# Lending a free layer-input block to the attention pipeline: one more buffer of parts, one more of transposed parts, and five units under way instead of four

## The chip, the core and the metric

The kernel runs on one core of one Trainium2 chip. The metric is the device time of one execution in microseconds (us). Five engines share the work: TensorE (PE in the profile; its weight loads are PEld), VectorE (DVE), ScalarE (ACT), GpSimd (POOL) and SyncE (SP). In this program SP issues nearly all transfers, from one queue, in the order in which they stand in it. PSUM is the memory that matmuls write; all else that is named here lies in SBUF.

## What is computed

Attention in which a query sees only keys of its own bucket, for 2 batches of 8 heads, 768 rows of 64 elements; then two layers on the 1536 x 512 result:

```
mask = q_bucket == k_bucket                   # six sign bits of a projection
scores = where(mask, q @ k.T / sqrt(64), -1e9)
attn = softmax(scores);  x = attn @ v          # put together to 1536 x 512
x = elu(x @ w_in) @ w_out                      # layer 1, 512 -> 2048 -> 512
r = relu(x @ w_in2);  y = (s * r * r + b) @ w_out2   # layer 2
```

Values are split into two f16 parts (high and low), and a product takes three f16 matmul passes: high by high, high by low, low by high.

## The kernel before

**Units.** A unit is one head by 128 queries; there are 96, and `u_s` to `u_av` (lines 378 to 441) take one through its steps. `u_s` makes the scores on PE (L384, four matmuls). `u_soft` takes the row minimum on DVE while it copies the scores to a buffer `p` (L395), scales the minimum (L396, on POOL for units 16 to 43), and takes the exponential on ACT (L397). From unit 16 on `u_split` writes the high part of the probabilities on ACT (L416) and the low part on POOL (L419) into a buffer of parts `ph`, which the SP queue transposes into a buffer `pt` (L421, a transfer). `u_av` multiplies `pt` by the values on PE (L440, 18 matmuls). After the eighth unit of a chunk of 128 rows `u_norm` divides by the sums on DVE, splits the result (L475 on POOL makes the low part), and transposes it into a block of layer input `xx[0]`, `xx[1]` or `xx[2]` (L479 for the first two chunks, L482 later). Each block holds four chunks, 8 KB in each of the 128 partitions. `xx[1]` is first written at the end of the fifth chunk, that is after unit 39.

**Buffers and units under way.** A small `Ring` object gives out the buffers of a kind in rotation. From unit 16 (`U0`) there are 3 `p`, 3 `ph` and 4 `pt`, and `attention` (line 518) issues the scores of a unit only while fewer than `nxt["lag"]` units lie between it and the last `u_av`: 4 from unit 16 on. When the stream of layer-1 weights is through, at unit 40 at the latest, `w1_step` adds one buffer of each kind and sets the lag to 5.

**Beside it.** Layer 1 (`moe1`, products at L574) works on blocks of two chunks, so its first block can start when the first two chunks are transposed. Its weights come as 64-bit numbers; `w_stream` loads them (L175 on SP, 512 KB each) and joins and splits them, mostly with four DVE instructions for a chunk (L213, L214, L216, L223). The layer's ELU takes a DVE instruction too (L591).

**What sets the order.** The Python code emits work in one sequence; a scheduler then places each instruction on its engine by priority and by when it reckons its inputs to be ready. Each engine runs its own list strictly in that order. Buffers and the lag enter the reckoning, so a change there moves instructions on all engines.

Of the kernel before, what the change touches and what calls it, by code (L numbers as in the profile page):

```python
# [7 lines left out]
F32 = mybir.dt.float32  # L8
# [10 lines left out]
PT = 4  # L19
EX = dict(p=1, ph=1, pt=1, raw=2)  # L20
NP = 3
# [17 lines left out]
NPH = 3  # L39
# [24 lines left out]
W_FROM = 3  # L64
HOLD = {(0, 2, "v"): 3, (0, 3, "v"): 4, (1, 0, "k"): 8, (1, 0, "q"): 9}
HOLD_E = []
LN2 = 0.6931471805599453


def model_kernel(tc, q, k, v, proj, w_in, w_out, w_in2, w_out2, s2, b2, sel, pop, eye, out):  # L70
    nc = tc.nc
    B, H, S, D = q.shape
# [22 lines left out]
    with ExitStack() as base:  # L95
# [13 lines left out]
        unp = right(ast, "unp", NP)  # L109
        un3 = right(ast, "un3", NPH)  # L110
        ptp = right(ast, "ptp", PT)
# [7 lines left out]
        class Ring:  # L119
            def __init__(self):  # L120
                self.sets, self.n = {}, {}
# [5 lines left out]
            def take(self, kind, shape, dt, name):  # L127
                pools = self.sets[kind]
                self.n[kind] += 1
                tag = "m" if kind == "w" else kind  # L130
                return pools[self.n[kind] % len(pools)].tile(shape, dt, tag=tag, name=name)

        class late_by:
            def __init__(self, n):
# [8 lines left out]
        ring = Ring()  # L143
# [22 lines left out]
        def behind(n):  # L166

            return tc.issue_after(w_loads[n]) if n is not None else nullcontext()
# [9 lines left out]
        def w_early(ch, x):  # L178
            t = xx[1].rearrange("p a t -> p (a t)").bitcast(I32)[:, 1024 * x:1024 * x + 1024]
            with behind(HOLD_E[x]):  # L180
                nc.sync.dma_start(out=t.rearrange("p (k n) -> p k n", k=ch[1].shape[1]), in_=ch[1])
            return ch, t.rearrange("p (n t) -> p n t", t=2)
# [192 lines left out]
        sps, pf, pt, sums, xacc = ({} for _ in range(5))  # L375
# [12 lines left out]
        def u_soft(u):  # L388
# [6 lines left out]
            nc.vector.tensor_scalar(f, sps.pop(u), CLAMP, None, op0=ALU.min, op1=ALU.min, accum_out=mx)  # L395
            (nc.gpsimd if U0 <= u < MXP else nc.vector).tensor_scalar(mx, mx, sm / (SQ * SQ), 10.0 * LN2, op0=ALU.mult, op1=ALU.add)  # L396
            nc.scalar.activation(out=f, in_=f, func=ACTF.Exp, scale=-sm / (SQ * SQ), bias=mx,  # L397
# [26 lines left out]
        def u_av(u):  # L424
            b, c, h, hp, j = unit(u)
            gr, sl = group(u)
            if sl == 0:
                xacc[gr] = ps_x.tile([128, H, D], F32, tag="x", name="xacc")
            acc = xacc[gr][:, sl, :]
            o = pt.pop(u)  # L430
            if u < FC * H:
                vv = raws[b, hp, "v"].rearrange("p h (c d) -> p h c d", d=D)
                for cc in range(C):
                    nc.tensor.matmul(acc, o[:, 128 * cc:128 * cc + 128], vv[:, j, cc, :],  # L434
                                     start=(cc == 0), stop=(cc == C - 1))
                return
            vv = vHL[b, hp]
            for z, (x, y) in enumerate(((0, 0), (0, 1), (1, 0))):
                for cc in range(C):
                    nc.tensor.matmul(acc, o[:, C * x + cc, :], vv[:, j, cc, y, :],  # L440
                                     start=(z == 0 and cc == 0), stop=(z == 2 and cc == C - 1))

        xx = [xs_.tile([128, 2 * KM, 512], F16, name=f"x{i}") for i in range(B * C // 4)]
# [68 lines left out]
        nxt = {"s": 0, "av": 0, "soft": [], "split": [], "lag": LAG0}  # L512
# [5 lines left out]
        def attention():  # L518
            for i in range(-PRE, 0):
                for fn, a in sched.get(i, []):  # L520
                    fn(*a)
                yield
            while nxt["av"] < NU:
                if nxt["split"]:
                    u_split(nxt["split"].pop(0), SPLIT(nxt["s"]))
                u = nxt["av"]
                if u < nxt["s"] and u in pt and (nxt["s"] - u >= nxt["lag"] or nxt["s"] == NU):
                    u_av(u)
                    nxt["av"] += 1
                    if u % H == H - 1:  # L530
                        u_norm(u // H)
                        if u >= FC * H - 1:
                            done_chunks[0] = u // H + 1
                u = nxt["s"]
                if u < NU and u - nxt["av"] < nxt["lag"]:
                    if u == U0:
                        ring.use(p=[unp], ph=[un3], pt=[ptp])
                        nxt["lag"] = PT
                    u_s(u)
                    nxt["s"] += 1  # L540
                    yield
                    u_soft(u)
                    nxt["split"].append(u)
                    for fn, a in sched.get(u, []):
                        fn(*a)
                yield
        att = attention()


# [302 lines left out]
        if True:  # L852
# [12 lines left out]
            n, early = 0, []  # L865
            co1 = w_col_chunks(lambda: wo, w_out)
            for _ in att:
                n += 1
                if len(early) < len(HOLD_E) and len(w_loads) > HOLD_E[len(early)]:
                    early.append(w_early(co1[len(early)], len(early)))  # L870
# [155 lines left out]
```

## Time and profile before

| what | value |
|---|---|
| median of 3 runs | 709.73 us (708.51 to 713.6) |
| profiled execution, its own time | 714.04 us |
| its span in the trace | 711.8 us |
| PE busy in the span | 659.6 us, 93% |
| DVE busy | 520.5 us, 73% |
| ACT busy | 416.3 us, 58% |
| POOL busy | 266.1 us, 37% |
| mean granted PE clock | 0.978 of full speed |

The span is what the trace covers; the execution's own time is 2.24 us longer. The trace's times count from the start of the span. The units that the change touches run from about 88 us (their first scores) to about 160 us (the last of their products). A busy PE is not PE at its peak, and idle time of an engine only costs where someone waits for it.

### The profile page before, as it was taken

The numbers are of one execution on the slowest core, as the hardware profiler recorded it, in microseconds if no ns is written. First come the engines' busy times: TensorE is split into PE (matmuls) and PEld (weight loads), VectorE is DVE, ScalarE is ACT, GpSimd is POOL, SyncE is SP. The second block draws the span as 40 slices with busy tenths as digits, with TensorE's granted clock in tenths as the row PEclk, the third lists the DMA queues.
The fourth block names the chain that finished last, engine by engine and source line by source line (L and its number), as shares of the span: only waits on it lengthen the run. The fifth ranks groups of instructions, "written<-read, shape, count | busy, mean of one in ns | idle before, by whom it ended". The sixth has DMA issues, their size and how long they took to land.

```text
span 711.8 us, 15212 instructions
## 1 busy us (share of the span) xinstructions
PE 659.6 (93%) x6192; PEld 506.6 (71%) x6192; DVE 520.5 (73%) x893; ACT 416.3 (58%) x687; POOL 266.1 (37%) x211
## 2 busy tenths in 40 slices
PE   2598978879989999999999999999999999999998
PEld 0286857668767777888888988874444446888887
DVE  5779989998878568645644699339999626999730
ACT  2849768966778788656755333234545525555520
POOL 0136767776345469945855421311211200000000
PEclk9769999999999999999999999999999999999999
DMA  9965699999999669977668555014443000000100
GB/s 211 299 162 170 160 203 203 223 228 225 196 211 216 116 116 171 150 125 122 119 115 117 135 162 165 1 31 119 135 138 112 0 1 1 16 31 31 45 30 30
DMA packets 206805, 89.72 MB, mean 126 GB/s; under 512 B 171920, under 2 KB 203408, under 8 KB 206736
## 3 DMA queue, kind: packets, MB, share of 16 engines
q1 hardware_dynamic: 206144, 88.63, 57.4%
q8 instruction: 48, 0.79, 0.5%
q14 instruction: 21, 0.17, 0.1%
q10 hardware_dynamic: 592, 0.14, 0.1%
HBM read 43.13 MB, written 3.15 MB: 65 GB/s over the span
## 4 chain that ended last, share of the span: by engine, by line
PE 66%; DMA 10%; DVE 10%; ACT 7%; issue 5%; SPq 1%; POOL 1%; DVEq 0%; ACTq 0%; POOLq 0%
PE h L574 27%; PE y L818 15%; PE x2p L574 12%; DMA pt<-ph 6%; PE s L384 4%; PE xacc L440 3%; PE xacc L434 2%; DVE p L395 2%; ACT p L397 1%; PE pT L406 1%; ACT ph L416 1%; DMA q<-src 1%; DVE g L591 1%; DMA raw<-in_k 1%; ACT q L357 1%
## 5 line engine op out<-in xcount | busy, mean ns | idle before, releaser
L419 POOL TENSOR_TENSOR ph<-p,ph 128x768 f16<-128x768 f32 x80 | 134.6, 1686 | 79.2 <-ACT ph L416 44.3
L574 PE MATMUL h<-x,wih 128*128 128x256 f16 x768 | 131.3, 275 | 3.0 <-DVE g L591 1.5
L574 PE MATMUL h<-x,wi 128*128 128x512 f16 x576 | 124.5, 379 | 0.0
L395 DVE TENSOR_SCALAR_CACHE_REDUCE p<-s 128x768 f32<-128x768 f32 x96 | 91.0, 951 | 42.2 <-PE s L384 41.3
L397 ACT ACTIVATE p<-p,mx 128x768 f32<-128x768 f32 x96 | 89.2, 929 | 50.6 <-DVE mx L396 38.8
L818 PE MATMUL y<-wqh,a 128*128 128x256 f16 x672 | 110.3, 273 | 0.0
L818 PEld LDWEIGHTS <-a 128*128 128x128 f16 x1008 | 98.6, 98 | 11.7
L574 PE MATMUL h<-x,wil 128*128 128x256 f16 x384 | 105.4, 275 | 0.0
L574 PE MATMUL x2p<-gh,woh 128*128 128x256 f16 x384 | 104.1, 273 | 0.8 <-ACT gh L594 0.8
L574 PE MATMUL x2p<-gl,woh 128*128 128x256 f16 x384 | 104.5, 273 | 0.1
L574 PEld LDWEIGHTS <-wi 128*128 128x128 f16 x576 | 56.4, 98 | 67.7
L574 PE MATMUL x2p<-gh,wol 128*128 128x256 f16 x384 | 104.5, 273 | 0.0
L818 PE MATMUL y<-wql,a 128*128 128x256 f16 x336 | 91.1, 273 | 0.0
L384 PE MATMUL s<-k,q 128*128 128x512 f16 (+1 forms) x384 | 80.7, 335 | 8.0 <-DVE p L395 7.9
L574 PEld LDWEIGHTS <-wih 128*128 128x128 f16 x768 | 74.9, 99 | 15.2 <-issue 2.0
L574 PEld LDWEIGHTS <-woh 128*128 128x128 f16 x768 | 74.9, 98 | 11.6
L597 POOL TENSOR_TENSOR gl<-g,gh 128x512 f16<-128x512 f32 x48 | 59.0, 1229 | 61.0 <-ACT gh L594 60.7
L440 PE MATMUL xacc<-vv,pt 128*128 128x64 f16 x1440 | 57.6, 194 | 16.1 <-DMA pt<-ph 16.1
L416 ACT ACTIVATE ph<-p 128x768 f16<-128x768 f32 x80 | 66.7, 836 | 7.7 <-DMA pt<-ph 5.2
L440 PEld LDWEIGHTS <-pt 128*128 128x128 f16 x1440 | 53.5, 99 | 24.3 <-DMA pt<-ph 20.3
L610 DVE SCALAR_TENSOR_TENSOR g<-h,sbs,r 128x512 f32<-128x512 f32 x48 | 35.7, 745 | 23.6 <-ACT r L607 23.6
L384 PEld LDWEIGHTS <-q 128*128 128x128 f16 x384 | 34.5, 100 | 25.6 <-issue 10.8
(118 smaller groups left out, 1040.8 us busy)
## 6 DMA issues: line engine op xcount, KB each, us to landing
wraw<-in_moe_w_in SPq DMA_DIRECT2D x32, 512.0 KB, 3.9
wraw<-in_moe_w_out SPq DMA_DIRECT2D x32, 512.0 KB, 3.9
out<-y SPq DMA_DIRECT2D x10, 256.0 KB, 2.0
raw<-in_k SPq DMA_DIRECT2D x6, 384.0 KB, 4.8
raw<-in_q SPq DMA_DIRECT2D x6, 384.0 KB, 5.7
v<-in_v SPq DMA_DIRECT2D x4, 384.0 KB, 7.8
pt<-ph SPq DMA_TRANSPOSE x80, 4.1
x<-in_k SPq DMA_DIRECT2D x2, 384.0 KB, 5.0
```

What stands on the lines that cost most here:

```text
L357: nc.scalar.activation(out=o[r, j].rearrange("p c t -> p (c t)"), in_=p[r], func=ACTF.Relu, scale=sc, bias=pop_sb[r, x:x + 1])
L384: nc.tensor.matmul(p[:, a0:a1], w[b, hp][:, j, c, :], kf[:, a0:a1], start=(x == 0), stop=(x == 1))
L395: nc.vector.tensor_scalar(f, sps.pop(u), CLAMP, None, op0=ALU.min, op1=ALU.min, accum_out=mx)
L397: nc.scalar.activation(out=f, in_=f, func=ACTF.Exp, scale=-sm / (SQ * SQ), bias=mx, accum_out=sums[gr][:, sl:sl + 1])
L416: nc.scalar.activation(out=t[:, 0, :], in_=f, func=ACTF.Copy)
L419: nc.gpsimd.tensor_tensor(out=t[:, 1, :], in0=f, in1=t[:, 0, :], op=ALU.subtract)
L434: nc.tensor.matmul(acc, o[:, 128 * cc:128 * cc + 128], vv[:, j, cc, :], start=(cc == 0), stop=(cc == C - 1))
L440: nc.tensor.matmul(acc, o[:, C * x + cc, :], vv[:, j, cc, y, :], start=(z == 0 and cc == 0), stop=(z == 2 and cc == C - 1))
L574: nc.tensor.matmul(p, ws[a](kk), xs[b](kk), start=(kk == 0 and z == 0), stop=(kk == n_kk - 1 and z == 2))
L597: nc.gpsimd.tensor_tensor(out=gl, in0=t["g"], in1=gh, op=ALU.subtract)
L610: nc.vector.scalar_tensor_tensor(out=g, in0=p, scalar=sb["s"], in1=t["r"], op0=ALU.mult, op1=ALU.mult)
L818: nc.tensor.matmul(p, a[:, xa, kk, :], wq[y][:, WQ[n], kk, :], start=first and k == 0, stop=k == 3 * K2 - 1, skip_group_check=True)
```

## The change

From unit 16 to unit 33 `Ring` gets a fourth buffer of parts `ph` and a fifth of transposed parts `pt`. Both lie in the block `xx[1]`, 3,072 bytes per partition each (`Guest` gives out a view of it). There is no fourth `p` (`X1["p"]` is 0). The lag is 5 from unit 16 and goes back to 4 at unit 34, when the rotations are set back to what they were. No instruction is added or removed: on each engine as many stand as before.

```
+X1 = dict(p=0, ph=1, pt=1)
+X1_END = 34
...
+        class Guest:
+            def __init__(self, t, at, n):
+                self.t, self.at, self.n = t, at, n
+            def tile(self, shape, dt, tag=None, name=None):
...
+                t = self.t[:, self.at // 2:(self.at + n * z) // 2]
...
                     if u == U0:
+                        t, at_, sets = xx[1].rearrange("p a t -> p (a t)"), 0, {}
+                        for k_, p_, n_ in (("p", unp, NP), ("ph", un3, NPH), ("pt", ptp, PT)):
+                            sets[k_] = [p_] * n_
+                            for _ in range(X1[k_]):
+                                sets[k_].append(Guest(t, at_, 4 * S))
+                                at_ += 4 * S
+                        ring.use(**sets)
+                        nxt["lag"] = PT + X1["pt"]
+                    if u == X1_END:
                         ring.use(p=[unp], ph=[un3], pt=[ptp])
                         nxt["lag"] = PT
```

In the lists below the changed kernel's line numbers are 19 higher for the lines that matter here: its L403, L415, L438, L440, L459, L494 and L498 are L384, L396, L419, L421, L440, L475 and L479 of before, and L194 is L175. A buffer that is written `x1_114` is the lent block.

**PE, where unit 16 comes to its product with the values** (`s` are scores, `k12` and `q12` head pair 2, `pt_967` the transposed parts of unit 16). Before, the end of the scores that stand ahead of it:

```order
L384 LDWEIGHTS q21_199
L384 MATMUL s_1034<-k21_189,q21_199 128x512
L384 LDWEIGHTS q21_199
L384 MATMUL s_1034<-k21_189,q21_199 128x256
L440 LDWEIGHTS pt_967
L440 MATMUL xacc_1094<-vv0_850,pt_967 128x64
```

and with the change:

```order
L403 LDWEIGHTS q12_356
L403 MATMUL s_1047<-k12_347,q12_356 128x512
L403 LDWEIGHTS q12_356
L403 MATMUL s_1047<-k12_347,q12_356 128x256
L403 LDWEIGHTS q22_358
L403 MATMUL s_1047<-k22_348,q22_358 128x512
L403 LDWEIGHTS q22_358
L403 MATMUL s_1047<-k22_348,q22_358 128x256
L459 LDWEIGHTS pt_967
L459 MATMUL xacc_1107<-vv0_850,pt_967 128x64
```

One more unit's scores stand ahead of the first product.

**POOL, where the second chunk's low part is made** (`xh` is the chunk's split result, `ph` or `x1` parts of a unit, `mx` the minimum). Before:

```order
L419 TENSOR_TENSOR ph_991<-p_986,ph_991 128x768
L396 TENSOR_SCALAR mx_1008<-mx_1008 128x1
L475 TENSOR_TENSOR xh_1029<-xf_1027,xh_1029 128x2x256
L396 TENSOR_SCALAR mx_1085<-mx_1085 128x1
L419 TENSOR_TENSOR ph_1012<-p_1007,ph_1012 128x768
L396 TENSOR_SCALAR mx_1133<-mx_1133 128x1
L419 TENSOR_TENSOR ph_1089<-p_1084,ph_1089 128x768
```

and with the change:

```order
L438 TENSOR_TENSOR ph_985<-p_980,ph_985 128x768
L415 TENSOR_SCALAR mx_1002<-mx_1002 128x1
L415 TENSOR_SCALAR mx_1022<-mx_1022 128x1
L438 TENSOR_TENSOR x1_114<-p_1001,x1_114 128x768
L438 TENSOR_TENSOR ph_1026<-p_1021,ph_1026 128x768
L494 TENSOR_TENSOR xh_1042<-xf_1040,xh_1042 128x2x256
```

The chunk's low part now stands behind the low parts of units 18 and 19.

**SP's queue at the same place.** Before:

```order
L421 DMA_TRANSPOSE pt_994<-ph_991 128x12x128
L175 DMA wraw_1178<-in_moe_w_out 128x4x256
L479 DMA_TRANSPOSE x0_113<-xh_1029 128x4x128 x2
L421 DMA_TRANSPOSE pt_1015<-ph_1012 128x12x128
L421 DMA_TRANSPOSE pt_1092<-ph_1089 128x12x128
```

and with the change:

```order
L440 DMA_TRANSPOSE pt_988<-ph_985 128x12x128
L194 DMA wraw_1191<-in_moe_w_out 128x4x256
L440 DMA_TRANSPOSE pt_1008<-x1_114 128x12x128
L194 DMA wraw_1293<-in_moe_w_out 128x4x256
L440 DMA_TRANSPOSE x1_114<-ph_1026 128x12x128
L498 DMA_TRANSPOSE x0_113<-xh_1042 128x4x128 x2
```

The chunk's two transposes into the layer input now stand behind two unit transposes and one more weight load.

## Rows read from the trace of the kernel before

**Rows 1.** The page: span and busy time of each engine.
```profile
span 711.8 us, 15212 instructions
PE 659.6 (93%) x6192; PEld 506.6 (71%) x6192; DVE 520.5 (73%) x893; ACT 416.3 (58%) x687; POOL 266.1 (37%) x211
```
**Rows 2.** Stretches: length, busy time by engine, granted PE clock, DMA share, GB/s.
```profile
110.00:155.00 45.00, 39.07 (x473) 31.90 (x470) 44.53 (x74) 37.55 (x68) 35.84 (x34) 1.00 1.06 213
155.00:170.00 15.00, 12.64 (x134) 9.98 (x133) 11.27 (x22) 9.53 (x18) 10.21 (x11) 0.89 1.13 242
170.00:181.00 11.00, 11.00 (x163) 9.73 (x162) 10.07 (x18) 6.08 (x11) 3.45 (x3) 1.00 1.12 202
181.00:300.00 119.00, 109.53 (x1321) 88.70 (x1317) 87.23 (x169) 98.79 (x168) 75.47 (x53) 1.00 0.93 168
300.00:445.00 145.00, 145.00 (x1662) 126.86 (x1661) 94.32 (x183) 75.92 (x130) 69.50 (x49) 1.00 0.65 132
```
**Rows 3.** Waits from 95 to 180 us: total us, times, longest.
```profile
PE xacc L440 <- DMA pt<-ph: 9.0, 7, 2.4
ACT ph L416 <- DMA pt<-ph: 2.8, 4, 1.1
```
**Rows 4.** Waits of SP's queue from 95 to 180 us, the first two.
```profile
SPq L421 <- POOL mx L396: 20.7, 11, 3.0
SPq L421 <- POOL ph L419: 8.0, 6, 2.1
```
**Rows 5.** PE in order of time: start, length, instruction, [idle before <- releaser].
```profile
97.09 1.14 PE L440 MATMUL xacc<-vv,pt 128*128 128x64 f16 x18 [2.01 <-DMA pt<-ph]
...
103.17 0.39 PE L574 MATMUL h<-x,wih 128*128 128x256 f16 x2 [1.48 <-DMA x<-xh]
...
160.17 0.70 PE L440 MATMUL xacc<-vv,pt 128*128 128x64 f16 x18 [2.36 <-DMA pt<-ph]
```
**Rows 6.** POOL in order of time: the second chunk's low part, unit 19's low part.
```profile
95.84 1.16 POOL L475 TENSOR_TENSOR xh<-xf,xh 128x512 f16<-128x512 f32 x1 [1.09 <-DVE xh L474]
...
99.69 1.65 POOL L419 TENSOR_TENSOR ph<-p,ph 128x768 f16<-128x768 f32 x1
```
**Rows 7.** SP's queue in order of time: the second chunk's transposes.
```profile
97.33 2.88 SPq L479 DMA_TRANSPOSE x<-xh  x2
```
**Rows 8.** PE in order of time: three units' scores, two units' products with the values.
```profile
90.88 2.11 PE L384 MATMUL s<-k,q 128*128 128x512 f16 x12
...
107.32 1.21 PE L440 MATMUL xacc<-vv,pt 128*128 128x64 f16 x36
```
**Rows 9.** DVE in order of time: the row minimum before unit 16's product, and waits.
```profile
95.67 0.95 DVE L395 TENSOR_SCALAR_CACHE_REDUCE p<-s 128x768 f32<-128x768 f32 x1
...
161.32 0.96 DVE L395 TENSOR_SCALAR_CACHE_REDUCE p<-s 128x768 f32<-128x768 f32 x1 [1.42 <-PE s L384]
...
167.62 0.96 DVE L395 TENSOR_SCALAR_CACHE_REDUCE p<-s 128x768 f32<-128x768 f32 x1 [1.45 <-PE s L384]
```
**Rows 10.** PE alone, slices of 1 us: length, busy, granted clock, DMA share, GB/s.
```profile
161.00:162.00 1.00, 1.00 (x7) 0.77 1.10 246
162.00:163.00 1.00, 1.00 (x17) 0.50 0.70 165
163.00:164.00 1.00, 1.00 (x12) 0.50 1.01 332
164.00:165.00 1.00, 1.00 (x7) 0.52 1.22 237
```
**Rows 11.** A slice of 0.5 us, columns as in rows 2.
```profile
143.00:143.50 0.50, 0.50 (x7) 0.45 (x5) 0.50 (x2) 0.00 (x0) 0.46 (x1) 1.00 1.28 284
```
**Rows 12.** Waits from 181 to 300 us.
```profile
PE xacc L440 <- DMA pt<-ph: 7.0, 7, 1.7
```
**Rows 13.** PE in order of time: layer products, three matmuls apart.
```profile
103.83 0.38 PE L574 MATMUL h<-x,wih 128*128 128x256 f16 x2
...
104.16 0.38 PE L574 MATMUL h<-x,wih 128*128 128x256 f16 x2
```

More of the change, by code (lines that the diff above doesn't have):

```diff
@@ L131, in take @@
                 return pools[self.n[kind] % len(pools)].tile(shape, dt, tag=tag, name=name)
+        class Guest:
+            def __init__(self, t, at, n):
+                self.t, self.at, self.n = t, at, n
+            def tile(self, shape, dt, tag=None, name=None):
+                z = 4 if dt == F32 else 2
+                n = 1
+                for d in shape[1:]:
+                    n *= d
+                assert n * z <= self.n
+                t = self.t[:, self.at // 2:(self.at + n * z) // 2]
+                t = t.bitcast(F32) if z == 4 else t
+                if len(shape) == 3:
+                    t = t.rearrange("p (a b) -> p a b", a=shape[1])
+                return t
         class late_by:
```

## The prediction, made before the changed kernel ran

> **What bounds the kernel now.** I read the page first. PE is busy 659.6 of 711.8 us and no other engine comes near [rows 1], so the time is PE's work plus the time in which PE stands still or runs at its lower clock. The change adds and removes no instruction; it can only move PE's idle time. The second view, busy time by stretch, says where there is any: from 300 to 445 us PE is busy for all of 145.00 us; from 110 to 155 it idles 5.9 of 45 us, from 155 to 170 2.4 of 15, from 170 to 181 not at all, from 181 to 300 9.5 of 119 [rows 2]. The lent buffers serve units 16 to 33, whose products with the values (L440) run from 97.09 to 160.17 us [rows 5], 17 unit periods of 3.71 us. So I look at that stretch, and then at what it hands on.
>
> The third view is the waits. Between 95 and 180 us PE waited seven times, 9.0 us in all, for a unit's transposed parts, at most 2.4 us [rows 3]; the first of these, 2.01 us at 97.09, is unit 16's own, whose transfer is issued as before [rows 5], so 7.0 us are open to the change. ACT waited four times, 2.8 us, for a free buffer of parts [rows 3]. The long waits of the transposes on SP's queue end with POOL's work, not with a product that frees a `pt` [rows 4]. So the fourth `ph` has a direct price in this trace, 2.8 us of ACT, and ACT is not full (37.55 of 45 us, rows 2); the fifth `pt` has none. What is left is the deeper pipeline: a product that comes later than its transpose.
>
> DVE is the other thing to see. From 110 to 155 us it is busy 44.53 of 45 us [rows 2]: there row minima and weight splitting are the pace, and units can't come faster than DVE passes them. From 155 to 170 it idles 3.7 us, of which 1.42 and 1.45 us are waits for scores [rows 9] that stand on PE behind the product that came late at 160.17.
>
> **The change part by part.**
>
> *Lead of the scores.* The lag goes up by one unit, but what counts is how many units' scores stand ahead of a product in PE's list. I counted that in both orders for units 16 to 33: before, 4.25 to 6, with the change 5 to 7; for units 17 to 33 the mean goes from 5.29 to 5.65. A product gets 0.36 unit, 1.3 us at 3.71 us a unit, more time for its transpose, not a unit. At unit 33, the late one, the lead goes from 4.5 to 5, 1.9 us.
>
> *Unit 16's product* now stands behind a fifth unit's scores. They need the minimum before them, which ends at 95.67 + 0.95 = 96.62 [rows 9], and take a third of 2.11 us [rows 8], so PE is through at 97.3 instead of having waited until 97.09 [rows 5]: +0.2 us, below what I can resolve; it counts as part of the next term.
>
> *The start of layer 1.* The second chunk's low part ran on POOL at 95.84 [rows 6], SP issued its transposes at 97.33 [rows 7], and PE's layer products had them at 103.17 after a wait of 1.48 us [rows 5]. Now the low part stands behind those of units 18 and 19, and unit 19's can't end before 99.69 + 1.65 = 101.34 [rows 6]. With 1.16 us for itself, SP gets the issue at 102.5 instead of 97.33: 5.2 us later, so the layer's products wait for 103.17 + 5.2 = 108.4 us. PE has more to do before them now: two more units' scores (2/3 of 2.11) and two products (1.21, rows 8) come from behind to ahead of them, 2.6 us. Idle there becomes 1.48 + 5.2 - 2.6 = 4.1 instead of 1.48: +2.6, with the fifth scores **+2.8 us**. Ends: 0, if the low parts of units 18 and 19 come sooner than they did, and +5.2 with none of the moved work in the gap, plus 1.7 for the clock (next) if the idle is long enough to lower it.
>
> *From 110 to 155 us.* 7.0 - 2.4 = 4.6 us of PE's waits for transposes lie here. What I weigh is whether they come back. The row of the stretch has DVE idle for 0.5 us [rows 2]; a unit that waits less for its transpose is still handed on at DVE's pace, so PE would stand at the next scores. I take **0**; the ends are -4.6 (all of it filled by layer products that stand in between) and +0.5 (the DVE slack lost too). The Trainium skill, Perfetto Trace Analysis, Identifying Performance Opportunities, says that improvement comes from the most-contended engine. By that rule the stretch gives nothing, since the change touches no DVE work; by PE's wait rows alone it would give 4.6.
>
> *From 155 to 170 us.* Unit 33's product waited 2.36 us [rows 5]. With 1.9 us more lead 0.5 is left. Behind that wait the granted clock fell from 2.4 to 1.2 GHz: 0.77 in the slice from 161 us, 0.50 in the next two, 0.52 in the one from 164 [rows 10], so 0.23 + 0.5 + 0.5 + 0.48 = 1.7 us of work lost; from 110 to 155 us, where the waits are shorter, the clock stays at 1.00 [rows 2]. DVE has 3.7 us of room here, so the gain can be kept. **-3.6 us.** Ends: 0 and -4.1.
>
> *From 181 us on.* The rotations are as before from unit 34, all lists are reshuffled, the work is the same. PE waits 7.0 us for transposes here [rows 12], and these can fall either way: **0**, ends -3.5 and +3.5 by half of that row.
>
> *Sum:* +2.8 + 0 - 3.6 + 0 = -0.8 us. Against the profiled execution's own 714.04 that is 713.2; that execution lies 4.3 above the median of 709.73, and above all three timed runs, so against the median I forecast **708.9 us**.
>
> **The rivals.**
>
> *The waits were a shortage of buffers.* All six remaining waits shrink by the 1.3 us of lead: the five before 155 us, 0.9 us each in the mean, vanish (4.6), the longest loses 1.3; the fall of the clock goes with them, 1.7; and the layer's start costs nothing. Then 709.73 - 7.6 = **702.1 us**. For it: the waits repeat, product after product, on the engine that should be full, and ACT's 2.8 us point to buffers too. Against it: DVE's 44.53 of 45. The Trainium skill, Perfetto Trace Analysis, Consistent bubbles under Identifying Performance Opportunities, reads a gap that repeats on the engine that should be saturated as a possible sign of too few buffers; the trace has such gaps, but no transpose that waited for a `pt`.
>
> *The queue takes the gain.* The DMA share is 1.06 and 1.13 in the two stretches [rows 2], and a slice in which transfers run without a gap has 1.28 [rows 11]. Units that come earlier find the weight loads in front of them, transposes only land later, and the product waits as long. Then only the start's 2.8 us are left: **712.5 us**. For it: 83% to 88% of that best slice. Against it: the 12% to 17% left.
>
> *Attention stays at DVE's pace and layer 1 falls behind: slower.* In PE's new order there are 24 to 64 fewer layer matmuls ahead of the scores of a given unit from the thirtieth on; at the sixtieth, whose scores lie in the last part of the stretch to 300 us, 758 instead of 803. If attention runs no faster, these 45 are done later, and from 300 us on PE is full and nothing hides them [rows 2]. Three take 0.33 us [rows 13], so 45 cost 4.95; with one more fall of the clock at the layer's start, 1.7, the time is 709.73 + 6.65 = **716.4 us**. It decides if attention reaches the sixtieth unit less than about 4 us sooner than before. For it: DVE full to 155 us. Against it: DVE's 3.7 us of room from 155 to 170, and near the end of attention the new order is only 12 matmuls behind.
>
> *The change doesn't do what it says* is half true already (0.36 unit of lead instead of one) and is in the forecast.
>
> **How the numbers follow.** Forecast, about 709 us: 0.47. Buffers, 702.1: 0.20. Queue, 712.5: 0.18. Layer behind, 716.4: 0.15. A measurement of this kernel can tell about 1% from no change, here 702.6 and 716.8. Faster by over 1%: half of the buffers' case and a little of the forecast's lower tail, 0.14. Slower by over 1%: half of the layer's case and the upper tails, 0.11. Within 1%: 0.75. All cases but the outer halves of the two extreme ones, with the ends of the terms, give 701 to 715.5 us as the range for 8 in 10.
>
> **What would show it.** In the new trace: the first long wait of layer products should end near 108 us, not 103, with 4 us of idle before it; if it ends by 104, the start's term is wrong. The waits of L440 between 110 and 155 us should shrink, while PE's idle time there stays near 6 us and moves to other releasers, with DVE still full; if PE's idle falls by 4, the DVE term is wrong. The wait near unit 33 should be under 1 us, with no clock of 0.5 behind it. PE's idle time up to 300 us, against that of before, tells the sum. It would be wrong altogether if a new fall of the clock, or a new order of the second batch's preparation after 181 us, moved more than 4 us.

## The result, and the profile after

The change is **slower by 1.0%**: 718.64 us (median of 8, 717.09 to 722.71) against 711.76 us for the kernel before (median of 8 beside it), ratio 1.0104 with the interval 1.0070 to 1.0138. The forecast was 708.9. Of the 9.7 us between, 2.0 lie in the level of before (709.73 in the three runs shown, 711.76 in eight) and 7.7 in the sum: -0.8 forecast, +6.9 measured.

The profiled execution of the change took 720.25 us, 6.2 more than that of before. Its page answers to [rows 1]:

```profile
span 718.5 us, 15207 instructions
PE 661.7 (92%) x6192; PEld 503.8 (70%) x6192; DVE 519.2 (72%) x893; ACT 415.4 (58%) x687; POOL 264.4 (37%) x211
```

The same work, then; PE is idle for 56.8 us of the span instead of 52.2. The stretches of [rows 2], with two more, in the change:

```profile
90.00:110.00 20.00, 13.62 (x139) 9.97 (x139) 19.86 (x33) 12.76 (x22) 12.74 (x14) 0.83 1.05 210
110.00:155.00 45.00, 37.98 (x470) 30.11 (x469) 41.72 (x73) 39.88 (x75) 37.06 (x35) 0.97 1.10 229
155.00:181.00 26.00, 25.81 (x313) 21.97 (x312) 21.78 (x40) 15.09 (x27) 11.06 (x12) 0.99 0.97 201
181.00:300.00 119.00, 108.53 (x1278) 86.58 (x1276) 80.84 (x154) 92.36 (x155) 69.66 (x48) 0.97 0.91 160
300.00:700.00 400.00, 396.69 (x3398) 296.25 (x3397) 281.01 (x439) 192.01 (x309) 95.88 (x65) 1.00 0.34 80
```

and in the kernel before, the three that [rows 2] do not have:

```profile
90.00:110.00 20.00, 15.23 (x175) 11.72 (x175) 16.52 (x30) 14.57 (x27) 13.22 (x14) 0.91 1.00 205
155.00:181.00 26.00, 23.64 (x294) 19.72 (x293) 21.34 (x39) 15.62 (x28) 13.66 (x14) 0.93 1.13 225
300.00:700.00 400.00, 399.02 (x3422) 299.06 (x3421) 280.21 (x432) 189.32 (x304) 92.94 (x62) 1.00 0.33 79
```

From each row I take one number, PE's **lost time**: length minus busy, plus (1 - granted clock) times length. (Idle time at a lowered clock counts twice in it; that is about a microsecond here.) Before and after: 6.6 and 9.8 us from 90 to 110; 5.9 and 8.4 to 155; 4.2 and 0.5 to 181; 9.5 and 14.0 to 300; 1.0 and 3.3 to 700. The sum from 90 us on goes from 27.2 to 36.0. Up to unit 16's product the lists of PE are the same; there this execution of the change was some 3 us ahead (unit 19's scores at 90.86 instead of 94.28 us), which is no gain of the change.

PE's waits from 95 to 180 us, which answer to [rows 3], and from 181 to 300, which answer to [rows 12]:

```profile
PE xacc L459 <- DMA pt<-ph: 5.2, 7, 2.4
PE h L602 <- DVE p L414: 3.0, 1, 3.0
PE xacc L459 <- DMA pt<-x: 1.5, 2, 1.1
PE xacc L459 <- DMA x<-ph: 1.1, 1, 1.1
...
PE xacc L459 <- DMA pt<-ph: 7.3, 6, 3.2
PE pone L372 <- DVE bits L362: 1.7, 1, 1.7
```

The waits for transposed parts became smaller in the stretch with the lent buffers (9.0 to 5.2 us, and 2.6 more for transposes out of or into the lent block, 7.8 together), a new wait of 3.0 us stands at the start, and after 181 us they are as before in sum but longer one by one (3.2 at most, not 1.7). One by one on PE, in order of time, to compare with [rows 5]:

```profile
94.12 0.70 PE L459 MATMUL xacc<-vv,pt 128*128 128x64 f16 x18 [0.26 <-DMA pt<-ph]
99.22 0.58 PE L602 MATMUL h<-x,wih 128*128 128x256 f16 x2 [3.02 <-DVE p L414]
105.55 0.39 PE L602 MATMUL h<-x,wih 128*128 128x256 f16 x2 [0.18 <-DMA x<-xh]
151.89 1.14 PE L459 MATMUL xacc<-vv,pt 128*128 128x64 f16 x18 [2.38 <-DMA pt<-ph]
209.16 0.70 PE L459 MATMUL xacc<-vv,pt 128*128 128x64 f16 x18 [3.25 <-DMA pt<-ph]
228.29 0.49 PE L372 MATMUL pone<-bits,sel_sb 128*128 128x512 f16 x2 [1.67 <-DVE bits L362]
305.47 0.27 PE L602 MATMUL x2p<-gl,woh 128*128 128x256 f16 x1 [1.13 <-POOL gl L625]
```

The rows at 94.12, 151.89 and 209.16 are the products of units 16, 32 and 44. How far attention has come is best read from DVE's normalisation, once for eight units: the chunks that end with units 23, 31, 39, 47, 55, 63 and 71, before

```profile
125.53 0.68 DVE L462 TENSOR_TENSOR xf<-xacc,rr 128x512 f32<-128x512 f32 x1
153.90 0.69 DVE L462 TENSOR_TENSOR xf<-xacc,rr 128x512 f32<-128x512 f32 x1 [0.19 <-PE xacc L440]
186.30 0.69 DVE L462 TENSOR_TENSOR xf<-xacc,rr 128x512 f32<-128x512 f32 x1
235.69 0.69 DVE L462 TENSOR_TENSOR xf<-xacc,rr 128x512 f32<-128x512 f32 x1
267.17 0.68 DVE L462 TENSOR_TENSOR xf<-xacc,rr 128x512 f32<-128x512 f32 x1
288.71 0.68 DVE L462 TENSOR_TENSOR xf<-xacc,rr 128x512 f32<-128x512 f32 x1
314.89 0.69 DVE L462 TENSOR_TENSOR xf<-xacc,rr 128x512 f32<-128x512 f32 x1 [0.66 <-PE xacc L440]
```

and in the change

```profile
120.96 0.68 DVE L481 TENSOR_TENSOR xf<-xacc,rr 128x512 f32<-128x512 f32 x1
145.58 0.69 DVE L481 TENSOR_TENSOR xf<-xacc,rr 128x512 f32<-128x512 f32 x1 [0.61 <-PE xacc L459]
182.09 0.69 DVE L481 TENSOR_TENSOR xf<-xacc,rr 128x512 f32<-128x512 f32 x1
237.51 0.69 DVE L481 TENSOR_TENSOR xf<-xacc,rr 128x512 f32<-128x512 f32 x1
265.48 0.69 DVE L481 TENSOR_TENSOR xf<-xacc,rr 128x512 f32<-128x512 f32 x1
289.96 0.68 DVE L481 TENSOR_TENSOR xf<-xacc,rr 128x512 f32<-128x512 f32 x1
319.50 0.69 DVE L481 TENSOR_TENSOR xf<-xacc,rr 128x512 f32<-128x512 f32 x1 [1.97 <-PE xacc L459]
```

Attention really ran faster: a chunk in 24.6 us instead of 28.4, and 8.3 us ahead at unit 31 (3 of them from the start of the execution). It is 4.2 ahead at 39, 1.8 behind at 47, 1.7 ahead at 55 and 4.6 behind at 71: half of the lead is spent between units 31 and 39, before 182 us, and the rest by unit 47.

The row at 99.22 is the largest single wait of the start, and it is not the one that I had forecast. The layer's first products land in a PSUM bank that the early scores used, and wait until DVE has taken the minimum of the last of them, now one unit more. DVE and POOL there, in the change:

```profile
94.11 1.80 DVE L242 SCALAR_TENSOR_TENSOR wil<-wa,wih 128x512 f16<-128x512 f32 x1
95.84 1.86 DVE L493 CAST xh<-xf 128x512 f16<-128x512 f32 x1
98.21 0.94 DVE L414 TENSOR_SCALAR_CACHE_REDUCE p<-s 128x768 f32<-128x768 f32 x1
```

```profile
93.73 1.64 POOL L438 TENSOR_TENSOR x<-p,x 128x768 f16<-128x768 f32 x1 [0.46 <-ACT x L435]
95.51 1.90 POOL L438 TENSOR_TENSOR ph<-p,ph 128x768 f16<-128x768 f32 x1
```

and the same two DVE operations before, when POOL was not beside the cast and for at most 0.1 us beside the other:

```profile
92.06 0.69 DVE L223 SCALAR_TENSOR_TENSOR wil<-wa,wih 128x512 f16<-128x512 f32 x1 [0.34 <-ACT wih L206]
...
95.33 0.42 DVE L474 CAST xh<-xf 128x512 f16<-128x512 f32 x1
```

In the new order POOL's low parts of units run beside them, and the two end 0.5 and 0.3 us after POOL's: 2.5 us more on DVE ahead of the minimum that ends at 99.15. Behind that wait PE ran at 1.2 GHz, and again behind those at 151.89, 209.16 and 228.29; one slice of each. Length, busy, granted clock, DMA share, GB/s, on PE alone:

```profile
99.00:100.00 1.00, 0.78 (x4) 0.50 1.01 161
...
152.00:153.00 1.00, 1.00 (x19) 0.50 1.22 339
...
210.00:211.00 1.00, 1.00 (x7) 0.50 1.21 254
...
231.00:232.00 1.00, 1.00 (x7) 0.50 1.19 213
```

### The profile page after: what moved, and what is told of

It is laid out like the page before. It is cut to its first block, busy times and chain, and to the rows that moved or that the text cites. A ratio compares the mean times of both kernels' runs of the same rounds, so it can differ in the third digit from the quotient of the medians.

```text
span 718.5 us, 15207 instructions
## 1 busy us (share of the span) xinstructions
PE 661.7 (92%) x6192; PEld 503.8 (70%) x6192; DVE 519.2 (72%) x893; ACT 415.4 (58%) x687; POOL 264.4 (37%) x211
## 3 DMA queue, kind: packets, MB, share of 16 engines
q1 hardware_dynamic: 206144, 88.63, 56.8%
## 4 chain that ended last, share of the span: by engine, by line
PE 54%; DVE 15%; DMA 11%; ACT 10%; issue 6%; POOL 2%; SPq 2%; DVEq 0%; ACTq 0%; POOLq 0%
PE h L602 21%; PE y L846 15%; PE x2p L602 9%; DMA pt<-ph 5%; PE s L403 3%; PE xacc L459 3%; ACT p L416 3%; DVE e L617 2%; DVE p L414 2%; ACT ph L435 2%; DVE g L619 2%; DVE wx L233 2%; DVE wx L232 1%; ACT gh L622 1%; ACT e L610 1%
## 5 line engine op out<-in xcount | busy, mean ns | idle before, releaser
L438 POOL TENSOR_TENSOR ph<-p,ph 128x768 f16<-128x768 f32 x76 | 127.4, 1679 | 77.0 <-ACT ph L435 50.5
L403 PE MATMUL s<-k,q 128*128 128x512 f16 (+1 forms) x384 | 81.7, 339 | 10.3 <-DVE p L414 10.1
L625 POOL TENSOR_TENSOR gl<-g,gh 128x512 f16<-128x512 f32 x48 | 56.5, 1180 | 67.2 <-ACT gh L622 66.9
L435 ACT ACTIVATE ph<-p 128x768 f16<-128x768 f32 x76 | 63.1, 835 | 11.9 <-DMA pt<-ph 9.1
L459 PE MATMUL xacc<-vv,pt 128*128 128x64 f16 x1386 | 54.7, 194 | 14.3 <-DMA pt<-ph 12.8
L459 PEld LDWEIGHTS <-pt 128*128 128x128 f16 x1386 | 50.9, 99 | 21.7 <-DMA pt<-ph 17.0
L403 PEld LDWEIGHTS <-q 128*128 128x128 f16 x384 | 34.8, 102 | 29.5 <-issue 14.7
```

What stands on the lines that cost most here:

```text
L403: nc.tensor.matmul(p[:, a0:a1], w[b, hp][:, j, c, :], kf[:, a0:a1], start=(x == 0), stop=(x == 1))
L435: nc.scalar.activation(out=t[:, 0, :], in_=f, func=ACTF.Copy)
L438: nc.gpsimd.tensor_tensor(out=t[:, 1, :], in0=f, in1=t[:, 0, :], op=ALU.subtract)
L625: nc.gpsimd.tensor_tensor(out=gl, in0=t["g"], in1=gh, op=ALU.subtract)
```

## The experiments

Each was timed beside the kernel before on the same chip. The theories, as they came up: **A**, what costs is that the lists of instructions put attention ahead of layer 1; **B**, the lent block itself; **C**, the units from 24 on that run five deep, and the return to four; **D**, any other lists than those of before lose; **E**, only lists that differ while the second batch is prepared; **F**, the collision at the start of layer 1. The table gives, for each, where its lists part from those of before, the ratio with its interval, and lost time from 90 to 181 us and from 181 to 700 in its one profile, worked out as above. The ratio is estimated from all runs and can differ from that of the medians by 0.2%. A profile is one execution and lies up to 4.4 us from its kernel's median (e14 above, e5 and e17 3.9 below), so the last two columns tell less than the ratio does. In e9 the last one leaves out some 1.5 us at a lowered clock, which its row to 445 us shows (0.99) and the row to 700 us rounds away.

| run | lists part from before | ratio | 90-181 | 181-700 |
|---|---|---|---|---|
| before | | | 16.7 | 10.5 |
| the change | unit 16 | 1.0104 (1.0070-1.0138) | 18.6 | 17.4 |
| e1 guests, four deep | not | 1.0025 (1.0002-1.0049) | 15.1 | 10.7 |
| e2 `pt` lent alone | unit 16 | 1.0113 (1.0084-1.0141) | 18.6 | 14.6 |
| e3 five from 24 | 24 | 1.0069 (1.0044-1.0093) | 17.3 | 13.1 |
| e4 five to 23 | 16 | 1.0183 (1.0138-1.0229) | 23.8 | 21.3 |
| e5 change, other bank | 16 | 1.0099 (1.0061-1.0136) | 15.3 | 15.9 |
| e6 before, other bank | 18 | 1.0100 (1.0066-1.0133) | 18.0 | 14.4 |
| e7 attention ahead | 24 | 1.0115 (1.0079-1.0151) | 22.1 | 12.2 |
| e8 five to 38 | 16 | 1.0104 (1.0067-1.0141) | 16.4 | 15.5 |
| e9 layer ahead | 38 | 1.0092 (1.0057-1.0127) | 17.6 | 13.7 |
| e10 small shuffle | hardly | 1.0005 (0.9981-1.0029) | 14.1 | 10.7 |
| e11 change, layer forward | 16 | 1.0126 (1.0085-1.0166) | 17.6 | 16.3 |
| e12 layer ahead, late | 65 | 1.0054 (1.0033-1.0076) | 15.1 | 13.3 |
| e13 layer behind, late | 65 | 1.0048 (1.0022-1.0074) | 16.5 | 11.6 |
| e14 layer behind from 46 | 46 | 1.0093 (1.0063-1.0124) | 17.7 | 18.2 |
| e15 near neutral | 38, little | 1.0022 (0.9997-1.0048) | 16.1 | 12.5 |
| e16 change, cast on ACT | 16 | 1.0080 (1.0053-1.0107) | 18.2 | 14.2 |
| e17 five from 28 | hardly | 1.0009 (0.9987-1.0030) | 16.2 | 10.7 |

**e1**, the buffers without the depth.

```diff
-                        nxt["lag"] = PT + X1["pt"]
+                        nxt["lag"] = PT
```

> Both lent buffers from unit 16 to 33, but four units under way, as before: PE's and DVE's lists are those of before, row for row, and only the buffer that a unit's parts and transposed parts lie in differs. Theory A (the deeper pipeline puts attention ahead of layer 1 in the lists, and the layer pays for it): the time of before, 711.8 us, within 2 us, with at most 1 us gained from ACT's 2.8 us of waits for a free buffer of parts. Rival B (the lent block itself costs: its buffers, or the waits that hang on them): about 718, as with the whole change. Rival C (the loss comes from unit 24 on, in the units that run five deep up to the return to four at unit 34): the time of before.

Measured 712.42 against 711.43 us. In its trace the operations of PE, DVE, ACT and POOL stand in the order of before throughout. Rival B falls as the cause of the loss: by themselves the fourth `ph` and the fifth `pt` bring nothing, and cost a quarter of a per cent here (0.02% to 0.49%). Its stretch from 181 to 300 us:

```profile
181.00:300.00 119.00, 109.40 (x1321) 88.28 (x1319) 86.98 (x167) 97.84 (x165) 77.14 (x52) 1.00 0.91 166
```

With the same lists the stretch from 181 to 300 us has the same 1321 matmuls as before and 9.6 us lost instead of 9.5; in the change it has 1278. Unit 33's product in this run, and the slice of PE behind it:

```profile
158.86 0.70 PE L459 MATMUL xacc<-vv,pt 128*128 128x64 f16 x18 [3.03 <-DMA pt<-ph]
```

```profile
159.00:160.00 1.00, 1.00 (x23) 1.00 1.28 287
```

It waits longer than in the profile of before [rows 5], and the clock stays up.

**e2**, the depth without the fourth buffer of parts.

```diff
-X1 = dict(p=0, ph=1, pt=1)
+X1 = dict(p=0, ph=0, pt=1)
```

> Only the buffer of transposed parts is lent, with five units under way; the fourth buffer of parts is left out. The lists of all engines are those of the change, but for names of buffers. Theories A and C: the loss stays, 717 to 719.5 us. Rival B, if the lent buffer of parts were at fault: back to about 712. If the buffer of parts is worth its 2.8 us of ACT's waits, this kernel is up to 2 us slower than the change.

Measured 718.81 us: the whole loss. Since only `ph` differs from the change, ACT's waits for it were worth nothing that these intervals can tell. The prediction's 2.8 us were too much in any case: of the four waits of before only one, 1.10 us at unit 31, fell in units 16 to 33. In the change there is none in them, and one of 3.29 us at unit 37 (161.36 us), after the lent buffers are given back.

**e3** and **e4**, the depth in the second half of the stretch or in the first.

```diff
 # e3, at unit 16: four; five from unit 24
-                        nxt["lag"] = PT + X1["pt"]
+                        nxt["lag"] = PT
+                    if u == 24:
+                        nxt["lag"] = PT + X1["pt"]
 # e4
-X1_END = 34
+X1_END = 24
```

> Both buffers are lent from unit 16, but a fifth unit goes under way only from unit 24 to 33. Layer 1 starts as before (48 of its matmuls ahead of unit 24's scores, as before, against 12 in the change), and at unit 44 it stands where it stood before (425 against 419; in the change 379). Theory A: the loss goes, 707 to 712 us, by 3.6 us better than before where unit 33's product no longer waits and the clock does not fall there, worse by what the 24 matmuls cost that the layer is behind at units 26 to 40. Rival C: the loss stays, 716 to 719 us, since the deep stretch up to 33 and the return to four are the same.

> Both buffers are lent from unit 16 and five units are under way, but only up to unit 23; from 24 on four and the old buffers. Layer 1 starts as late as in the change (12 matmuls ahead of unit 24's scores) and falls as far behind (360 ahead of unit 44's, 745 ahead of unit 60's, against 379 and 758 in the change, 419 and 803 before). Theory A: as slow as the change or slower, 718 to 724 us. Rival C: the loss is mostly gone, 711 to 715 us, since the units from 24 on run as before.

Measured 717.07 and 724.71 us. e4 is as A had it, 0.7 us above its range, and C falls: without any deep unit after 23 the loss is larger. e3 is a miss for A: the layer starts as before and has caught up in the list by unit 44, yet two thirds of the loss remain.

**e5** and **e6**, the two early PSUM pools in the other order, so that the layer's first products land in other banks; in the change and, as control, before.

```diff
+        ps_p = [pool(st0, "ps_p0", P0, space=PSUM)]
         ps_s = [pool(st0, "ps_s0", S0, space=PSUM)]
-        ps_p = [pool(st0, "ps_p0", P0, space=PSUM) if P0 else ps_s[0]]
```

> The change, with the two early PSUM pools (of scores, and of bits and transposes) allocated in the other order, so that the first products of layer 1 no longer land in the bank of the fifth unit's scores, whose row minimum DVE read only at 98.21 us in the trace of the change (a wait of 3.02 us, and the clock at 1.2 GHz behind it); in PE's list 12 of those products now stand ahead of unit 20's scores. Theory A1 (the largest piece of the loss is this wait at the start of layer 1, some 3 to 4.5 us with the clock): 714 to 716 us against 718.7 of the change. Theory A2 (the start does not matter, the layer falls behind later all the same): 717.5 to 720. In either case the attention stays ahead in the list up to unit 45 as in the change, so a time below 713 would speak against theory A as a whole.

> The kernel before with the same other order of the two early PSUM pools; the control of the run with the change. Before, the first layer products did not wait for a bank (they started at 98.05 us behind unit 16's product). Theories A1 and A2: 710 to 713 us, no difference that can be told from 711.5. If the new order of the lists alone (12 products ahead of unit 20's scores, 24 fewer ahead of units 44 to 60) moves the time as the change does, 714 to 717.

Measured 718.9 and 718.27 us. In e5 the wait for the bank is gone (lost time from 90 to 181 us 15.3 instead of 18.6, in an execution 3.9 us below the median), and the time is that of the change all the same. The control is the surprise, and it lies above every range that was given for it: the kernel before, with its banks exchanged and its lists moved by this, loses what the change loses. What the banks themselves add in e6 is not told apart from the lists.

**e7**, attention put ahead with four units under way and nothing lent; **e8**, five deep up to 38.

```diff
 # e7, in the kernel before
-            credit = 0.0
+            credit, owed = 1.9, -1.3
...
+                if nxt["s"] >= 60:
+                    credit, owed = credit + owed, 0.0
 # e8
-X1_END = 34
+X1_END = 39
```

> The kernel before, with no lent buffer and four units under way; only the credit that decides how many steps of attention come between two groups of layer products starts 1.9 higher, and 1.3 is taken back from unit 60 on. The lists then have 12 to 41 fewer layer products ahead of the scores of units 24 to 42 (271 instead of 312 at unit 40, 300 instead of 330 at unit 42), as many as before from 44 to 60 (801 at 60, 803 before), and 16 to 24 fewer at the end of attention. Theory A (attention put ahead of layer 1 costs, whatever puts it there): 714 to 718 us, near the run with five units from 24 on (717.1). Rival C (the five units under way cost, not the place of the layer): 710 to 713 us.

> The change with the lent buffers and five units under way up to unit 38 instead of 33; at unit 40 the next lending with five units follows in any case, so the return to four lasts one unit. Theory A: the layer stands a little further back than in the change (264 of its products ahead of unit 40's scores against 270, 746 ahead of unit 60's against 758, 12 fewer at the end): the time of the change or up to 2 us more, 718 to 721 us. Rival C (the return to four at unit 34 makes the loss): 711 to 714 us.

Measured 719.57 and 718.28 us: neither depth nor the return to four is needed for the loss. Both have the direction that A asks for, e7 by 1.6 us more than its range; they fit D as well.

**e9** and **e10**, made to part A from D; **e11**, the change with the layer brought forward.

```diff
 # e9, in the kernel before
-            credit = 0.0
+            credit, owed = -1.3, 1.3   # and the two lines of e7
 # e10, in the kernel before: credit = -0.6;  e11, in the change: credit = -1.3
```

> The kernel before, without any lent buffer and with four units under way, the credit of attention started at -1.3 and given back from unit 60 on: the lists are those of before up to unit 38, and from there layer 1 stands up to 20 of its products further ahead (1.3 units' worth of credit; 823 instead of 803 ahead of unit 60's scores, 12 more at the end). Theory A (what costs is attention put ahead of the layer): not slower than before, 709 to 712.5 us. Theory D (the five engines' lists of before happen to fit each other; any other order loses, whichever of the two parts it puts ahead): 715 to 719 us.

> The kernel before with the credit of attention started at -0.6: nothing is lent, four units are under way, and the lists differ little; layer 1 stands within 6 products of before ahead of every unit up to 65 and 12 products further ahead from unit 70 on (a unit of attention is about 24). Theory A: the time of before, 711.5 us, within 1.5. Theory D in its strong form (any other order loses): 715 to 718 us.

> The change with the credit of attention started at -1.3: the start of layer 1 up to unit 36 is that of the change, and from unit 38 on the layer stands 16 to 30 products further ahead (261 against 229 at unit 38, 774 against 758 at unit 60, 36 more at 70). Theory A: the part of the loss that comes after 181 us goes, 714 to 716.5 us. Theory D: no better than the change, 717.5 to 721 us.

Measured 718.72, 712.21 and 719.63 us. **Theory A falls**: putting the layer ahead (e9) costs as much as putting it behind, and bringing it forward in the change (e11) gives nothing back. D holds, but not in its strong form: a small departure is free. e9 has the lists of before up to unit 38, at 159 us, but for a few products on PE, and what it loses more than before it loses after 181 us:

```profile
155.00:181.00 26.00, 23.81 (x291) 19.60 (x288) 23.48 (x38) 17.02 (x30) 11.58 (x12) 0.93 1.08 216
181.00:300.00 119.00, 107.63 (x1287) 86.55 (x1285) 85.94 (x165) 96.17 (x163) 73.48 (x51) 1.00 0.88 163
300.00:445.00 145.00, 142.84 (x1625) 123.77 (x1623) 93.25 (x179) 74.35 (x128) 67.93 (x47) 0.99 0.63 128
```

4.0 us lost from 155 to 181, as before (4.2); 11.4 against 9.5 to 300; and 2.2 idle plus a clock of 0.99 in the stretch to 445 in which PE was full before [rows 2].

**e12** to **e15**, one number each in the kernel before, which move its lists at other places.

```diff
 # e12 and e14
-STEP_COST = 2.5
+STEP_COST = 2.6   # e14: 2.4
 # e13, written as e7: credit, owed = 0.0, 2.5, given from unit 64 on
 # e15
-SC0 = 1.2
+SC0 = 1.3
```

> The kernel before with the price of a step of attention 2.6 instead of 2.5: the lists stand as before, by the layer's products, up to unit 65 (about 285 us), and from there layer 1 gets ahead by 36 of its products at unit 70 and 48 at the end. Theory E (the loss is made between 175 and 260 us): 710 to 713 us. Theory D (any other order loses): 715 to 720 us.

> The kernel before with 2.5 of credit given to attention once unit 64's scores are out: the lists stand as before up to there, by the layer's products, and from unit 70 on layer 1 is 24 of its products behind. Theory E: 710 to 713 us, as PE is full from 300 us on in either order. Theory D: 715 to 720 us.

> The kernel before with the price of a step of attention 2.4 instead of 2.5: as before up to unit 44 (about 205 us), then layer 1 falls behind, by 20 of its products at unit 52, 29 at 55, 24 at 70 and 60 at the end. Theory E: part of the loss, 712.5 to 716 us. Theory D: 715 to 720 us. If some orders gain as well as lose, below 710.

> The kernel before with the price of the first steps of attention 1.3 instead of 1.2: as before up to unit 38 (about 175 us), 11 layer products behind at unit 40, 10 ahead at 42, within 5 from 44 to 62, 16 to 36 ahead after unit 70. Theory E: 712 to 715 us, since little changes in the stretch that decides. Theory D: 715 to 720 us.

Measured 714.91, 714.98, 718.58 and 713.34 us against 711.44. E falls: e12 and e13, whose lists part only at about 280 us in the traces, still lose half a per cent. So does D's strong form again (e15). By and large the loss grows with how early and how far the lists part, but not in step: e3 parts at unit 24 and loses less than e14, which parts at 46. None gains.

**e16**, theory F; **e17**, five deep with nearly the lists of before.

```diff
 # e16, in the change
-            if FC <= ch < C:
+            if 1 <= ch < C:
 # e17: as e3, with unit 28 in place of 24
```

> The change, with the high part of the second chunk of layer input (L493) made on ACT instead of DVE: the 1.86 us that DVE spent on it beside POOL's low part lie no longer in front of the row minimum for which PE's first layer products waited. Theory F (the start of layer 1 is the largest piece of the loss, and it is this collision): the wait of 3.02 us falls under 1.5 us and the time to 714 to 716.5 us. Theory D (lists that part from those of before lose at one place or another; the layer here is up to 33 of its products further ahead at unit 38): the wait may go, but the time stays 717 to 721 us.

> The change with both buffers lent from unit 16, but a fifth unit under way only from unit 28 to 33. Before unit 28 the lists are those of before, and after it they are, but for names of buffers, those of the small shuffle (credit -0.6, 712.2 us): within 6 layer products up to unit 65, 12 ahead after. Theories D and F: 711 to 713.5 us, no difference from before or from the small shuffle. If five units under way, or the lent buffers in use while they are, cost by themselves: 715 to 719 us.

Measured 717.28 and 714.25 us against 712.92. In e16 the cast no longer stands on DVE, and PE's wait is 1.12 us instead of 3.02, but others follow at once:

```profile
96.03 0.38 PE L602 MATMUL h<-x,wih 128*128 128x256 f16 x2 [1.12 <-DVE p L414]
98.61 0.70 PE L459 MATMUL xacc<-vv,pt 128*128 128x64 f16 x18 [1.11 <-DMA pt<-x]
...
109.50 0.70 PE L459 MATMUL xacc<-vv,pt 128*128 128x64 f16 x18 [2.32 <-DMA pt<-ph]
```

Lost time from 90 to 181 us is 18.2, in the change 18.6, and the ratio, 1.0080, lies within the interval of the change: this wait is mostly gone, and most of the loss stays. The kernel before stood 1.4 us higher in these runs, so e16 lies 5.7 us above it by the ratio and 4.4 by the medians, at the border between the ranges of F and D: that a fifth of the loss hangs on this place is neither shown nor excluded. e17 clears the depth and the lent buffers together: with the lists nearly kept, five units under way cost nothing that can be told (714.25 is over the 713.5 expected by less than the kernel before stood higher). Up to about 282 us the operations of DVE, ACT and POOL stand in the order of before in e10 and in e17; after that layer 1 is 12 products ahead in both, and that is free, where the 24 to 48 products of e12 and e13 are not.

**What is settled and what is open.** Of 17 kernels, the three whose lists stay nearest to those of before (e1, e10, e17) lie between 1.0005 and 1.0025, and in their profiles, as before, lost time after 181 us is 10.5 to 10.7 us. Of the other 14, e15, which stays near, has 12.5 us and a ratio of 1.0022; thirteen are slower by 0.5% to 1.8%, with 11.6 to 21.3 us. None is faster, whichever part is put ahead. So the loss is one of the order, and adds up from several waits at places that differ from kernel to kernel. Which property of the lists of before makes them better was not found, so the cause inside the order stays open; that the five engines' lists have been fitted to each other is only an argument.

## Why the prediction was wrong, step by step

**The step that failed is "From 181 us on"**: "all lists are reshuffled, the work is the same", so 0, with ends of ±3.5 us by half of [rows 12]. Lost time after 181 us went from 10.5 to 17.4 us, and to 14.6 in e2, which has the same lists: +6.9 and +4.1. Two spells at 1.2 GHz make 3.6 us of the 17.4; e2's execution had none there. (That +6.9 is also the whole measured loss is chance: from 90 to 181 us 1.9 us more were lost as well, and this execution was 3 us ahead when that stretch began.) Neither the middle nor the ends were right. Twelve other reshuffles lost too; a reshuffle was no coin toss here. [Rows 12] could not bound it either: their sum hardly moved (7.0 to 7.3 us), but single waits became longer (3.25 us at unit 44) and new ones came at places where PE had not waited before (228.29, 305.47), with two spells of the lowered clock behind them.

*Unit 16's product* had waited 2.01 us and now waits 0.26 [rows 5]: the fifth scores stand in that wait, as forecast, with 1.38 us ahead of them for a row minimum.

*The start of layer 1*, +2.8 us, was right in size by luck (6.6 to 9.8 us lost, +3.2; e2 +3.6) and wrong in the wait. POOL's low part of the chunk ran at 97.77 us, since those of units 18 and 19 came sooner than the sum had them; its transposes went out only at 101.72, behind unit 19's on SP's queue. But PE had other work until 105.55 us and waited 0.18 us for them, not 4.1. The 3.02 us at 99.22 were for the bank of the fifth unit's scores and for DVE, slowed beside POOL; I had moved POOL's instructions in the sum, and not asked what DVE does beside them.

*From 110 to 155 us*, 0: measured +2.5 (e2 +1.7). The reason given, that units can't come faster than DVE passes them, took DVE's work between two units as fixed. It is not: the chunk from unit 24 to 31 took 24.6 us, not 28.4. Two rows with the columns of [rows 2], from the normalisation ahead of that chunk to its own, before and in the change; and a row of L223, the last step of weight splitting, from 110 to 155 us before (count, busy us, mean ns of one, idle us):

```profile
125.53:153.90 28.37, 25.00 (x314) 20.43 (x312) 27.97 (x49) 23.51 (x44) 22.83 (x22) 1.00 1.07 226
120.96:145.58 24.62, 20.55 (x272) 16.17 (x270) 22.91 (x41) 21.98 (x41) 20.81 (x22) 1.00 1.12 231
...
L223 DVE SCALAR_TENSOR_TENSOR wol<-wa,woh 128x512 f16<-128x512 f32 x9 | 11.2, 1247 | 0.0
```

DVE was busy for 22.91 us of that chunk instead of 27.97, with 20 instructions of weight splitting instead of 25. DVE had been full because splitting comes with the layer's steps, and fewer of these stood between the units in the new order. And part of its busy time was itself waiting: L223 took 1.25 us in the mean, and 0.69 where no POOL operation ran beside it, so about 5 of the 44.53 us (an estimate from these rows). Whether DVE still set the pace of the faster chunk no run here tests. By the rule of the Trainium skill (Perfetto Trace Analysis, Identifying Performance Opportunities) the most-contended engine is the one to relieve; the trace has its busy time as I read it, but that time did not say what a unit costs there.

*From 155 to 170 us*, -3.6: unit 33's own wait is gone, as forecast (its product runs at 155.35 us without one), but unit 32, which had not waited, now waits 2.38 us at 151.89, with the lowered clock behind it. The wait moved by a unit; lost time from 110 to 181 us together fell from 10.1 to 8.9 us (e1, with the lists of before: 9.6), by 1.2 and not by 3.6. And the clock's 1.7 us, which I had tied to that wait, are not tied to it: in e1, with the lists of before, unit 33 waited 3.03 us and the clock stayed at 1.00.

*The rivals.* The shortage of buffers is out by e1, e2 and e17. The queue's time, 712.5, would be 714.6 from the level of 711.76, below the interval of the change (716.7 to 721.6), so it is not the whole; unit transposes did land later after their issue (medians of 5.2 to 5.4 us from 95 to 160 us, before 4.7), and what that cost no run tests. "Layer 1 falls behind" had the time almost exactly, +6.65 against +6.9, and its own condition was met: attention was 1.7 us ahead at unit 55 and 1.3 behind at 63, so less than 4 ahead at 60. But its reason does not hold by itself. Attention was up to 8.3 us ahead on the way, and with the layer ahead the kernel before loses as much (e9), while bringing it forward in the change gives nothing back (e11). That 45 products stood behind at unit 60 says how much PE had lost by then, not why. The sentence of the forecast on what would make it "wrong altogether", a new fall of the clock or a new order after 181 us of more than 4 us, is what happened; it had been given no chance of its own.

## What to carry to other kernels

Where a change moves an order that several engines follow in step, cost the move itself: a few moves of the same size that do nothing else tell its price (here between nothing, for the smallest, and 1.8%, never a gain), and the new resource without the new order (e1) tells in one run which of the two matters. An engine that is busy all the time in a stretch may be so with work of another stream, and in part with waiting inside its instructions; follow the units through the stretch before taking its busy time as what they cost.

## What the hardware showed that was not expected

- The cast of 128x512 took 0.42 us on DVE and 1.86 us beside a POOL operation that ended 0.29 us earlier; the product with a scalar and two SBUF operands (L223, L242 in the change) took 0.69 and 1.80 us. The row minimum took 0.94 to 0.96 us in either case. The Trainium skill, SBUF — State Buffer, Who interferes with whom, states that a DVE operation in a two-port mode (a cast can be in one) excludes a GpSimd operation for the whole instruction, and that one with two SBUF inputs contends with a GpSimd operation that reads SBUF. The trace agrees for these two, and not for every operation with two SBUF inputs: the joins of the weights' halves (L214 and L216, L233 and L235 in the change, two SBUF inputs of int32) took 0.63 to 0.71 us in both traces, also where a POOL operation ran beside them for all of it (L216 at 136.62 us before: 0.68 us, beside a low part from 136.49 that took 1.65).
- A wait of 2.36 us at unit 33 before had the clock at 1.2 GHz behind it [rows 10]; one of 3.03 us at the same unit, with the same lists, had not (e1).
